# State products and scores of a state attention with an MoE-style layer, moved from 128x32 to 64x32 array tiles

## The chip, the cores and the metric

The kernel runs on one core of a Trainium2 chip. The metric is device time in microseconds (us) of one execution; for the kernel before, three runs are at hand. The profile is one execution recorded by the hardware profiler. PE is the matrix engine (matmuls; PEld is its weight loads), DVE the vector engine, ACT the scalar engine, POOL the general engine; SP issues most DMAs.

## What is computed

For each of 8 batches and 8 heads, 512 tokens `x` and 32 state rows `state` (64 values each) read each other by softmax attention; the 544 results per batch, 512 wide over the heads, go through a layer norm and a two-layer network with a residual.

```python
scores = x @ state.T / 8;          a = softmax(scores);   xread = a @ state      # 512 x 32 per head
scores2 = state @ x.T / 8;         a2 = softmax(scores2); sread = a2 @ x         # 32 x 512 per head
x2 = concat([xread, sread])        # heads side by side: (8, 544, 512)
xn = (x2 - mean) / sqrt(var + 1e-6) * g_ln
out = x2 + relu(xn @ w_ch1) @ w_ch2     # w_ch1 512 x 2048, w_ch2 2048 x 512, both float64 in memory
```

## The kernel before

All operands of large products are split into a high and a low float16 part, and a product is the sum of three of the four part products (`TERMS`). The two weight matrices are loaded as 64-bit words and cut to 32 bits on the chip; they are handled in four units `u` of 512 hidden columns. `weights1(u)` loads w1 (`raw`, 2 DMAs of 1 MB), converts it (`words`), multiplies by the gain and subtracts the column mean, finds a scale and splits (`split`) to float16; four DMAs (`w1c<-raw`) then copy the parts to tile `w1c` so that the high half of a head's 64 rows and the low half lie on the 128 partitions one above the other. `weights2(u)` does the same for w2 and needs no copies.

For a token, `xread` is a softmax row times the 32 state rows, so the first layer is taken through the state: `state_products(b)` (L660) multiplies the state (`sT`, weights in the array) by w1 once per batch, `matrix` = state x w1, 256 rows (8 heads x 32) by 512 columns per unit, and the layer's products then use `matrix` with the softmax numerators `ea`. In `state_products` and in `scores` (L400) the array is cut into four tiles of 128 rows and 32 columns, one for each of four heads `j`; the 128 rows hold a head's high and low halves stacked. For one half `g` of the heads, `a` = 0, 1 (state high, state low) times four heads makes 8 matmuls of 512 columns (L665, L403). Each group writes one PSUM bank from a pool of two (`half`); the bank is evicted by one ACT and one DVE instruction into `matrix`.

`read_state` (L475) does `a2 @ x` with 32 matmuls of 64 columns per batch; since the halves of x lie on separate output rows, ACT copies the result to SBUF and four float32 matmuls with a matrix `fold` (L492) add the halves and turn rows and columns.

For batch 0 the first layer (L701) and second layer (L715) are plain; from batch 1 on they are done with a Strassen-like scheme (`strassen_hidden`, L799, and `strassen_products`, L855) that uses 7 instead of 8 products with combinations of w2 (L747, tile `sums`). The last stage takes the 256 rows of `sread` (all batches) through the same layers (`first_of_state`, L808), for which two DMAs per unit (`high<-w1c`) copy w1's high halves to another layout.

Every piece of work is a step of a numbered stream, and the text `PLAN` lists stream:step pairs in the order in which they are issued; each engine executes its own steps in that order, so a step that waits holds up what stands behind it on its engine. Waits on data and on free tiles are put in by the tile framework. `banks` is a pair of PSUM banks with one buffer, used in a batch by the scale search, `scores`, `read_state` and the mix of token reads (L515). `accumulator` has four banks.

## Time and profile before

| what | value |
|---|---|
| runs | 666.45, 667.62, 667.91 us (median 667.62) |
| profiled execution, span | 665.9 us (the page gives no other time for it) |
| busy: PE, DVE, ACT, POOL | 626.3, 498.0, 388.2, 216.7 us |
| PE busy in 0 to 80 us, in 150 to 620 us | 48.1 of 80, 468.1 of 470 us |
| HBM read and written | 28.05 and 9.44 MB |

The page gives busy times by engine, busy tenths in 40 slices of the span, the chain of work that ended last, groups of like instructions with mean duration and the idle time before them, and DMA issues. The rows on which the argument stands are shown with the prediction. In rows of a group, the two shapes behind a name are the output and the input; for PE, `128*32` is rows times columns of the array that the instruction uses.

### The profile page before, as it was taken

To read this page: it belongs to the slowest core of one execution; us is meant where nothing else is said; L and a number is where in the kernel's file an instruction comes from. 1 tells how busy PE (TensorE), PEld (TensorE's weight loads), DVE (VectorE), ACT (ScalarE), POOL (GpSimd) and SP (SyncE) were. 2 spreads that over 40 slices of the span, in tenths; PEclk is the share of its full clock that TensorE was granted. 3 is DMA by queue.
4 is the path that set the end of the run, shared out by engine and by line. 5 is a ranking of instruction groups with operands and counts; after the bars stand their busy time and mean duration, and the time that the engine had idled before them with its cause. 6 is when DMAs were issued, how large, how long until landed. Compare 5 with 4: busy or idle time off the path is not lost.

```text
span 665.9 us, 14680 instructions
## 1 busy us (share of the span) xinstructions
PE 626.3 (94%) x5948; PEld 493.1 (74%) x5948; DVE 498.0 (75%) x1002; ACT 388.2 (58%) x699; POOL 216.7 (33%) x189
## 2 busy tenths in 40 slices
PE   0676999999999999999999999999999999999996
...
PEclk9977999999999999999999999999999999999998
...
DMA packets 98563, 69.63 MB, mean 105 GB/s; under 512 B 72704, under 2 KB 90624, under 8 KB 98048
## 3 DMA queue, kind: packets, MB, share of 16 engines
...
q10 hardware_dynamic: 1248, 0.79, 0.4%
...
HBM read 28.05 MB, written 9.44 MB: 56 GB/s over the span
## 4 chain that ended last, share of the span: by engine, by line
PE 90%; DVE 5%; DMA 2%; ACT 1%; issue 1%; DVEq 0%; SPq 0%
PE acc L855 41%; PE half L799 22%; PE acc L715 6%; PE half L665 5%; PE acc L701 3%; PE half L808 3%; PE acc L747 2%; PE acc L599 2%; PE banks L403 1%; DVE w_t L186 1%; PE banks L479 1%; PE banks L515 1%; PE banks L492 1%; DMA x_f<-in_x_dram 1%; PE acc L608 1%; DMA w1c<-raw 1%
## 5 line engine op out<-in xcount | busy, mean ns | idle before, releaser
L855 PEld LDWEIGHTS <-xs 128*128 128x128 f16 x2520 | 242.4, 98 | 43.6 <-issue 15.3
L186 POOL TENSOR_TENSOR xs<-rs,xs 128x512 f16<-128x512 f32 x120 | 142.4, 1199 | 272.7 <-ACT xs L186 207.1
L855 PE MATMUL acc<-w2h,xs 128*128 128x256 f16 x1440 | 183.0, 273 | 0.0
L799 PE MATMUL half<-ea,matrix 128*128 128x256 f16 x1344 | 159.4, 273 | 0.0
L799 PEld LDWEIGHTS <-matrix 128*128 128x128 f16 x1344 | 130.7, 98 | 16.6 <-issue 0.8
L855 PE MATMUL acc<-sums,xs 128*128 128x256 f16 x1080 | 141.9, 273 | 0.0
L186 DVE SCALAR_TENSOR_TENSOR rs<-half,rs 128x256 f32<-128x256 f32 x224 | 89.4, 419 | 27.6 <-ACT rs L186 13.3
L186 ACT ACTIVATE xs<-rs 128x512 f16<-128x512 f32 x128 | 77.1, 618 | 40.5 <-DVE rs L186 33.8
L186 ACT ACTIVATE xs<-half 128x256 f16<-128x256 f32 (+1 forms) x112 | 53.6, 487 | 72.5 <-PE half L799 50.5
L186 DVE SCALAR_TENSOR_TENSOR xs<-half,xs 128x256 f16<-128x256 f32 (+1 forms) x112 | 61.2, 550 | 28.1 <-ACT xs L186 24.5
L186 ACT ACTIVATE matrix<-half,hs 128x512 f16<-128x512 f32 x56 | 38.0, 687 | 35.2 <-PE half L665 34.9
L186 DVE SCALAR_TENSOR_TENSOR matrix<-half,hs,matrix 128x512 f16<-128x512 f32 x56 | 41.2, 742 | 16.0 <-ACT matrix L186 15.3
L186 ACT ACTIVATE rs<-half 128x256 f32<-128x256 f32 x56 | 21.3, 381 | 42.5 <-PE half L799 40.1
L715 PE MATMUL acc<-w2h,hid 128*128 128x512 f16 x192 | 43.1, 379 | 0.0
L186 DVE TENSOR_TENSOR strip<-acc,strip 128x256 f32<-128x256 f32 (+1 forms) x60 | 33.2, 554 | 10.5 <-PE acc L855 7.5
L665 PE MATMUL half<-w1c,sT 128*32 128x512 f16 x448 | 33.5, 384 | 1.9 <-DVE rs L186 1.0
L186 POOL TENSOR_TENSOR ts<-ts,mA 128x1024 f32<-128x1024 f32 (+1 forms) x8 | 14.4, 1804 | 60.9 <-DVE mA L186 54.5
L715 PEld LDWEIGHTS <-hid 128*128 128x128 f16 x192 | 18.5, 98 | 20.9 <-issue 0.4
L186 DVE SCALAR_TENSOR_TENSOR x<-x_f,x_s,x 128x512 f16<-128x512 f32 x32 | 24.8, 798 | 5.3 <-ACT x L186 5.3
L186 DVE BATCH_NORM_STATS2 s<-xr 128x6 f32<-128x512 f32 x32 | 21.6, 684 | 8.7 <-ACT xr L186 8.6
L186 ACT ACTIVATE x<-x_f,x_s 128x512 f16<-128x512 f32 x32 | 21.7, 713 | 9.8 <-DVE x_s L186 9.8
L186 POOL TENSOR_TENSOR hid<-strip,hid 128x512 f16<-128x512 f32 x16 | 18.5, 1170 | 26.6 <-ACT hid L186 26.5
(152 smaller groups left out, 770.1 us busy)
## 6 DMA issues: line engine op xcount, KB each, us to landing
raw<-in_moe_w_ch_dram SPq DMA_DIRECT2D x9, 1024.0 KB, 7.3
out_dram<-xr SPq DMA_DIRECT2D x16, 512.0 KB, 3.0
x_f<-in_x_dram SPq DMA_DIRECT2D x15, 512.0 KB, 5.6
sums<-in_moe_w_ch_dram SPq DMA_DIRECT2D x7, 1024.0 KB, 8.2
...
ek<-ek SPq DMA_DIRECT2D x7, 512.0 KB, 4.3
xr<-part POOLq DMA_DIRECT2D x6, 512.0 KB, 5.0
w1c<-raw SPq DMA_DIRECT2D x8, 256.0 KB, 5.1
```

The lines of the kernel that those rows point to most:

```text
L186: return lambda: f(*map(now, args), **{k: now(v) for k, v in kw.items()})
L403: nc.tensor.matmul(o[32 * j:32 * j + 32], lhsT=sT[:, g, a, 32 * j:32 * j + 32], rhs=xT[:, s, 4 * g + j].rearrange("p c t -> p (c t)"), sta ...
L479: nc.tensor.matmul(ps_z[:, h // 4, :, h % 4], lhsT=xv[:, c // hc, h, c % hc], rhs=ebT[:, :, h // 4, c, 32 * (h % 4):32 * (h % 4) + 32], st ...
L492: nc.tensor.matmul(pr[:, g], lhsT=z4[:, g, i], rhs=fold, start=i == 0, stop=i == 1, skip_group_check=True)
L599: nc.tensor.matmul(ps, lhsT=gm[:, k:k + 1].broadcast_to([P, P]), rhs=t4[:, k], start=k == 0, stop=k == 3)
L665: nc.tensor.matmul(ps[32 * j:32 * j + 32], lhsT=sT[:, g, a, 32 * j:32 * j + 32], rhs=w[:, 2 * g + j // 2, j % 2], start=a == 0, stop=a == ...
L701: nc.tensor.matmul(o[:, 256 * f:256 * f + 256], lhsT=m[:, g, i, P * (q + f):P * (q + f) + P], rhs=ea[:, s, k, g], start=f == 0 and g == 0 ...
L715: nc.tensor.matmul(po, lhsT=hid[:, i, q, c * P:(c + 1) * P], rhs=w[:, j, q], start=first and q == 0 and n == 0, stop=last and q == 3 and n ...
L747: nc.tensor.matmul(o, lhsT=signs[:, k // 2], rhs=v[k], start=start and k == 0, stop=k == 3, skip_group_check=True)
L799: nc.tensor.matmul(ps[:, 256 * q:256 * q + 256], lhsT=m[:, h, i, P * (2 * k + q):P * (2 * k + q) + P], rhs=ea[:, 0, j, h, 256 * g:256 * g ...
L808: nc.tensor.matmul(ps[:, 256 * q:256 * q + 256].rearrange("p (t n) -> p t n", t=2), lhsT=w[:, k // 2, k % 2, fs] if k < H else wn[:, k - H ...
L855: nc.tensor.matmul(po[o], lhsT=y[:, n, i, o] if o < 2 else x[:, o - 2, n, i], rhs=v[j], start=u == 0 and n == 0 and k == 0 and o in (2, 1, ...
```

## The change

Row halves. w1's rows now come in by head half: partitions 0 to 63 hold heads 0 to 3, partitions 64 to 127 heads 4 to 7. Each raw load becomes two DMAs of 64 partitions (8 more DMAs in all), the gain is loaded in two pieces, and `split` writes `w1c` directly: the 16 copies `w1c<-raw` and `w1c<-sums` and the 8 copies `high<-w1c` are gone. `x16` and `xT` take the same layout; the state's `sT` is built with one ACT and one DVE instruction in place of one and two.

Tiles. `scores` and `state_products` use tiles of 64 rows and 32 columns: 8 tiles (two row halves `g`, four columns `j`), three sets of part products, 24 matmuls of 512 columns for what took 16 in four sets. The two halves `g` write different PSUM banks. From batch 1 on the products of a unit are taken into the pair `banks` instead of two tiles of `half`, and are evicted by one ACT and one DVE instruction of 1024 columns.

State reads. `read_state` uses 48 matmuls (three part products summed in PSUM), then ACT and DVE copy 64 partitions each to SBUF, and one float32 transpose on PE takes the place of the four float32 products.

Order. `PLAN` is a new table throughout. Three places follow.

On DVE in the start-up, the rows up to the first units of `matrix` of batch 0 (`ts`, `dA`, `ef` and `ea` belong to the softmax, `raw`, `sums` and `w1c` with `w1_t` are the low parts of w1's units, `w1_t` with `gx` the gain and mean). Before:

```order
L186 SCALAR_TENSOR_TENSOR raw_147<-w1_t_155,of_weights_216,raw_147 128x2048
L186 SCALAR_TENSOR_TENSOR raw_247<-w1_t_183,of_weights_216,raw_247 128x2048
L186 SCALAR_TENSOR_TENSOR w1_t_351<-w1_t_351,gx_77,acc_424 128x512 x4
L186 TENSOR_REDUCE dA_241<-ts_205 128x16
L186 TENSOR_SCALAR dA_241<-dA_241 128x16
L186 SCALAR_TENSOR_TENSOR sums_70<-w1_t_139,of_weights_216,sums_70 128x2048
L186 RECIPROCAL dA_241<-dA_241 128x16
L186 SCALAR_TENSOR_TENSOR matrix_470<-acc_440,matrix_470 128x512
```

Now:

```order
L192 SCALAR_TENSOR_TENSOR w1c_294<-w1_t_160,of_weights_247,w1c_294 128x2048
L192 TENSOR_TENSOR ts_251<-ts_251,dA_308 128x512
L192 STREAM_TRANSPOSE ef_342<-ts_251 128x512
L192 SCALAR_TENSOR_TENSOR w1_t_314<-w1_t_314,gx_77,acc_319 128x512
L192 TENSOR_REDUCE dA_308<-ts_251 128x16
L192 TENSOR_SCALAR dA_308<-dA_308 128x16
L192 RECIPROCAL dA_308<-dA_308 128x16
L192 SCALAR_TENSOR_TENSOR ea_381<-ef_342,ea_381 128x512
L192 SCALAR_TENSOR_TENSOR matrix_385<-acc_346,matrix_385 128x512
L192 SCALAR_TENSOR_TENSOR matrix_385<-acc_347,matrix_385 128x512
```

Before, three units of w1 are split ahead of the first `matrix`; now one is, and the other two stand some ten rows behind it.

On SP's queue in the start-up, the w1 loads up to the first transposes. Before:

```order
L186 DMA s_j_75<-in_state_dram 128x2x64
L585 DMA sums_70<-in_moe_w_ch1_dram 128x2x1024 x2
L585 DMA raw_147<-in_moe_w_ch1_dram 128x2x1024
L585 DMA raw_157<-in_moe_w_ch1_dram 128x2x1024
L585 DMA raw_173<-in_moe_w_ch1_dram 128x2x1024
L186 DMA_TRANSPOSE xT_178<-x16_108 128x16x128
```

Now:

```order
L192 DMA s_j_75<-in_state_dram 128x2x64
L584 DMA sums_70<-in_moe_w_ch1_dram 64x2x1024 x4
L584 DMA raw_137<-in_moe_w_ch1_dram 64x2x1024 x2
L584 DMA raw_152<-in_moe_w_ch1_dram 64x2x1024 x2
L584 DMA raw_164<-in_moe_w_ch1_dram 64x2x1024 x2
L584 DMA raw_180<-in_moe_w_ch1_dram 64x2x1024 x2
L192 DMA_TRANSPOSE sT_0_198<-sh_96 128x2x128
```

Six megabytes in twelve DMAs, before five in five, go out ahead of the first transpose.

On DVE in a later batch, around evictions of `matrix` (`rs` and `xs` are the Strassen combinations). Before:

```order
L186 SCALAR_TENSOR_TENSOR eb<-eB,eb 128x1024
L186 SCALAR_TENSOR_TENSOR matrix<-half,hs,matrix 128x512
L186 SCALAR_TENSOR_TENSOR xs<-half,xs 128x2x256
L186 TENSOR_REDUCE dA<-ts 128x32
L186 TENSOR_SCALAR dA<-dA 128x32
L186 RECIPROCAL dA<-dA 128x32
L186 SCALAR_TENSOR_TENSOR matrix<-half,hs,matrix 128x512 x2
```

Now, at a place where two units follow each other closely:

```order
L192 SCALAR_TENSOR_TENSOR matrix<-banks,hs,matrix 128x2x512
L192 TENSOR_SCALAR ux<-x_i 128x1
L192 SCALAR_TENSOR_TENSOR rs<-half,rs 128x256 x2
L192 SCALAR_TENSOR_TENSOR xr<-strip,of_second,xr 128x512
L192 SCALAR_TENSOR_TENSOR matrix<-banks,hs,matrix 128x2x512
```

One instruction of 1024 columns from `banks` stands for two of 512 from `half`, and the next unit's products wait for it, since the pair has one buffer.

The diff (of the table two rows are shown; where `...` stands, lines that follow from these are left out):

```diff
--- before.py
+++ after.py
-    "1:0 1:3-4 1:1-2 1:5-12 4:1 1:19 1:72 0:0 4:6 1:20 1:24-25 4:5 4:7 4:0 4:3 1:17-18 4:2 4:4 3:1 3:6 1:22-23 "
+    "0:0 1:4 1:3 1:2 1:1 1:0 1:5-11 4:0-1 1:13 1:12 1:18 1:71 2:0 1:14 1:23 1:21 4:2-3 1:19 1:24 1:22 4:6 4:4-5 2:1 "
...
-            yield do(engines[hh].dma_start, out=xf[:, hs], in_=src[:, hs])
+            o, i = (xf[:, hh], src[:, :, 2 * hh:2 * hh + 2]) if b == 0 else (xf[:, 0, hs], src[:, hs])
+            yield do(engines[hh].dma_start, out=o, in_=i)
...
-        sT = fixed([P, G, 2, P], F16, f"sT_{b % 2}")
-        yield do(nc.scalar.activation, sh[:, :, 0], sj.unsqueeze(2).broadcast_to([P, G, 2, D]), AF.Copy, scale=sst)
-        for i in range(2):
-            yield do(nc.vector.scalar_tensor_tensor, sh[:, :, 1, i], sj, sst, sh[:, :, 0, i], ALU.mult, ALU.subtract)
-        yield do(nc.sync.dma_start_transpose, out=sT.rearrange("p g a n -> p (g a) n"),
-                 in_=sh.rearrange("p g a i d -> p (g a i d)"))
-
-        xT = (rows("xT") if b > 0 else unit(3, "xT")).bitcast(F16).rearrange("p (s h c t) -> p s h c t", s=parts, h=H, c=hc)
-        xTa = xT.rearrange("p s h c t -> p (s h c) t")
+        sT = fixed([P, 2, P], F16, f"sT_{b % 2}")
+        yield do(nc.scalar.activation, sh[:, 0], sj, AF.Copy, scale=sst)
+        yield do(nc.vector.scalar_tensor_tensor, sh[:, 1], sj, sst, sh[:, 0], ALU.mult, ALU.subtract)
+        yield do(nc.sync.dma_start_transpose, out=sT, in_=sh.rearrange("p i g d -> p (i g d)"))
...
-        def scores(s, g, o, sT, xT):
-            for a in range(2):
+        def scores(s, ps, sT, xT):
+            for n, (a, i) in enumerate(TERMS):
                 for j in range(4):
-                    nc.tensor.matmul(o[32 * j:32 * j + 32], lhsT=sT[:, g, a, 32 * j:32 * j + 32],
-                                     rhs=xT[:, s, 4 * g + j].rearrange("p c t -> p (c t)"),
-                                     start=a == 0, stop=a == 1, skip_group_check=True)
-
-        psv = ps if parts == 1 else ps.rearrange("p s (g t) -> p g s t", g=G)
-        eB = quad("eB").rearrange("p (g s t) -> p g s t", g=G, s=parts)
+                    for g in range(G):
+                        k = hc * (4 * s + j)
+                        nc.tensor.matmul(ps[32 * j:32 * j + 32, g, w * s:w * s + w],
+                                         lhsT=sT[D * g:D * g + D, a, 32 * j:32 * j + 32],
+                                         rhs=xT[D * g:D * g + D, k:k + hc, i], start=n == 0, stop=n == 2,
+                                         skip_group_check=True)
...
         def read_state(ps_z, x16, ebT):
-            xv = x16.rearrange("p (s h c) i d -> p s h c (i d)", s=parts, c=hc)
-            for h in range(H):
+            for j in range(4):
                 for c in range(C):
-                    nc.tensor.matmul(ps_z[:, h // 4, :, h % 4], lhsT=xv[:, c // hc, h, c % hc],
-                                     rhs=ebT[:, :, h // 4, c, 32 * (h % 4):32 * (h % 4) + 32],
-                                     start=c == 0, stop=c == C - 1, skip_group_check=True)
+                    a = hc * (4 * (c // hc) + j) + c % hc
+                    for n, (i, k) in enumerate(TERMS):
+                        nc.tensor.matmul(ps_z[:, j], lhsT=x16[:, a, i], rhs=ebT[:, k, :, c, 32 * j:32 * j + 32],
+                                         start=c == 0 and n == 0, stop=c == C - 1 and n == 2, skip_group_check=True)
         yield do(read_state, ps_z, x16, ebT)
-        z = halves("z").bitcast(F32)[:, 0:512]
-        z4 = z.rearrange("p (g i n) -> p g i n", g=G, i=2)
-        pr = pz[:, 1, 0:G * D].rearrange("p (g d) -> p g d", g=G)
+        z = halves("z").bitcast(F32)[:, 0:P]
+        pr = pz[:, 1, 0:G * D]
         sread = fixed([P, G, D], F32, "sread")
-        yield do(nc.scalar.activation, z, pz[:, 0], AF.Copy)
-
-        def fold_halves(pr, z4):
-            for g in range(G):
-                for i in range(2):
-                    nc.tensor.matmul(pr[:, g], lhsT=z4[:, g, i], rhs=fold, start=i == 0, stop=i == 1,
-                                     skip_group_check=True)
-        yield do(fold_halves, pr, z4)
-        yield do(nc.vector.tensor_tensor, sread, pr, rB.unsqueeze(2).broadcast_to([P, G, D]), ALU.mult)
+        for g, copy in enumerate((partial(nc.scalar.activation, func=AF.Copy), nc.vector.tensor_copy)):
+            r = slice(D * g, D * g + D)
+            yield do(copy, z[r].rearrange("p (j n) -> p j n", j=4), ps_z[r, :, g])
+        yield do(nc.tensor.transpose, pr, z, idf)
+        yield do(nc.vector.tensor_tensor, sread, pr.rearrange("p (g d) -> p g d", g=G),
+                 rB.unsqueeze(2).broadcast_to([P, G, D]), ALU.mult)
...
-            nc.sync.dma_start(out=raw.rearrange("p (k f) -> p k f", k=2),
-                              in_=w1[256 * fh:256 * fh + 256, 1024 * u:1024 * u + 1024].rearrange("(k p) f -> p k f",
-                                                                                                  p=P))
+            rows_of = w1[:, 1024 * u:1024 * u + 1024].rearrange("(g j d) f -> g d j f", g=G, j=4)
+            for g in range(G):
+                nc.sync.dma_start(out=raw[D * g:D * g + D].rearrange("p (k f) -> p k f", k=2),
+                                  in_=rows_of[g, :, 2 * fh:2 * fh + 2])
...
-        hl = raws[1].bitcast(F16).rearrange("p (i e) -> p i e", i=2)
-        yield from split(hl[:, 0], hl[:, 1], t, scale)
-        hl = hl.rearrange("p i (k f) -> p i k f", k=4)
-        w = narrow(u, "w1c").bitcast(F16).rearrange("p (k s f) -> p k s f", k=4, s=2)
-        w1c[u] = w
-        for i in range(2):
-            for s in range(2):
-                to = 64 * (i ^ s)
-                yield do(nc.sync.dma_start, out=w[to:to + 64, :, s], in_=hl[64 * s:64 * s + 64, i])
+        w = narrow(u, "w1c").bitcast(F16).rearrange("p (i e) -> p i e", i=2)
+        yield from split(w[:, 0], w[:, 1], t, scale)
+        w1c[u] = w.rearrange("p i (j f) -> p i j f", j=4)
...
-        def multiply(ps, g, sT, w):
-            for a in range(2):
+        def multiply(ps0, ps1, sT, w):
+            for n, (a, i) in enumerate(TERMS):
                 for j in range(4):
-                    nc.tensor.matmul(ps[32 * j:32 * j + 32], lhsT=sT[:, g, a, 32 * j:32 * j + 32],
-                                     rhs=w[:, 2 * g + j // 2, j % 2], start=a == 0, stop=a == 1, skip_group_check=True)
+                    for g in range(G):
+                        nc.tensor.matmul((ps0, ps1)[g][32 * j:32 * j + 32],
+                                         lhsT=sT[D * g:D * g + D, a, 32 * j:32 * j + 32],
+                                         rhs=w[D * g:D * g + D, i, j], start=n == 0, stop=n == 2, skip_group_check=True)
         sT = results[b][1]
         for u in range(U):
             m = matrix[b][u] = block(4, f"matrix_{u}", 1, "matrix").bitcast(F16).rearrange("p (g i f) -> p g i f", g=G, i=2)
-            for g in range(G):
-                ps = accumulator() if b == 0 else half()
-                scale = CM if b == 0 else hs[:, u:u + 1]
-                yield do(multiply, ps, g, sT, w1c[u])
-                yield do(nc.scalar.activation, m[:, g, 0], ps, AF.Copy, scale=scale)
-                yield do(nc.vector.scalar_tensor_tensor, m[:, g, 1], ps, scale, m[:, g, 0], ALU.mult, ALU.subtract)
+            scale = CM if b == 0 else hs[:, u:u + 1]
+            if b == 0:
+                ps = [accumulator() for _ in range(G)]
+                todo = [(ps[g], m[:, g, 0], m[:, g, 1]) for g in range(G)]
+            else:
+                two = banks()
+                ps = [two[:, g] for g in range(G)]
+                todo = [(two, m[:, :, 0], m[:, :, 1])]
+            yield do(multiply, *ps, sT, w1c[u])
+            for v, hi, lo in todo:
+                yield do(nc.scalar.activation, hi, v, AF.Copy, scale=scale)
+                yield do(nc.vector.scalar_tensor_tensor, lo, v, scale, hi, ALU.mult, ALU.subtract)
...
-                def first_of_state(ps, j, w, wn, xsT):
+                def first_of_state(ps, k, w, xsT):
                     for q in range(2):
-                        fs = slice(P * (2 * j + q), P * (2 * j + q) + P)
-                        for k in range(12):
-                            nc.tensor.matmul(ps[:, 256 * q:256 * q + 256].rearrange("p (t n) -> p t n", t=2),
-                                             lhsT=w[:, k // 2, k % 2, fs] if k < H else wn[:, k - H, fs], rhs=xsT[:, :, k],
-                                             start=q == 0 and k == 0, stop=k == 11, skip_group_check=True)
+                        fs = slice(P * (2 * k + q), P * (2 * k + q) + P)
+                        for n, (i, a) in enumerate(TERMS):
+                            for j in range(4):
+                                nc.tensor.matmul(ps[:, 256 * q:256 * q + 256].rearrange("p (t n) -> p t n", t=2),
+                                                 lhsT=w[:, i, j, fs], rhs=xsT[:, :, 4 * a + j],
+                                                 start=q == 0 and n == 0 and j == 0, stop=n == 2 and j == 3,
+                                                 skip_group_check=True)
...
-    def high_halves(u):
-
-        high[u] = quad("high").bitcast(F16).rearrange("p (k f) -> p k f", k=4)
-        for s in range(2):
-            half = slice(64 * s, 64 * s + 64)
-            yield do(nc.sync.dma_start, out=high[u][half], in_=w1c[u][half, :, s])
+    state_rows_T = [None]
...
```

81 lines of the change are left out of this document (41 added, 40 removed), and 243 rows, old and new, of the table PLAN.

## Prediction, written before the changed kernel was run

> **What bounds the kernel now.** I read the page's busy times and slices first, then the stretches, then single rows on PE.
>
> ```profile
> PE 626.3 (94%) x5948; PEld 493.1 (74%) x5948; DVE 498.0 (75%) x1002; ACT 388.2 (58%) x699; POOL 216.7 (33%) x189
> PE   0676999999999999999999999999999999999996
> PEclk9977999999999999999999999999999999999998
> 0.00:20.00 20.00, 4.58 (x8) 2.16 (x9) 12.66 (x30) 10.21 (x16) 0.70 (x6) 1.00 0.92 325
> 20.00:40.00 20.00, 14.35 (x61) 5.91 (x59) 18.40 (x32) 11.72 (x13) 0.00 (x0) 0.83 1.00 321
> 40.00:60.00 20.00, 12.02 (x118) 6.80 (x118) 18.92 (x27) 17.26 (x22) 1.05 (x1) 0.79 0.89 199
> 60.00:80.00 20.00, 17.18 (x173) 11.86 (x172) 17.44 (x38) 17.34 (x29) 5.59 (x5) 0.87 0.89 248
> 150.00:620.00 470.00, 468.12 (x4753) 391.91 (x4746) 354.51 (x737) 261.13 (x507) 172.55 (x144) 1.00 0.32 78
> ```
>
> In a stretch's row, busy time stands in the order PE, PEld, DVE, ACT, POOL, then granted clock, DMA share and GB/s. From 80 us on PE is the bound: 468.1 of 470 us in the long stretch, at clock 1.00, with DVE at 75% and ACT at 56% there. Before 80 us PE lies idle 31.9 us (80 less 48.1), while DVE is busy 67.4 of 80. So two currencies count: PE time taken out of the steady part, at face value as long as the other engines follow; and in the start-up the time at which DVE has prepared enough for PE.
>
> **Tiled products.** This piece of PE's timeline shows what a tiled step costs.
>
> ```profile
> 214.15 0.62 PE L665 MATMUL half<-w1c,sT 128*32 128x512 f16 x8
> 214.70 1.48 PE L855 MATMUL acc<-w2h,xs 128*128 128x256 f16 x12
> 216.02 0.82 PE L855 MATMUL acc<-sums,xs 128*128 128x256 f16 x6
> 216.77 0.62 PE L665 MATMUL half<-w1c,sT 128*32 128x512 f16 x8
> 217.32 1.11 PE L479 MATMUL banks<-ebT,x 128*128 128x64 f16 x32
> 218.35 0.61 PE L665 MATMUL half<-w1c,sT 128*32 128x512 f16 x8
> ...
> 86.50 1.05 PE L665 MATMUL half<-w1c,sT 128*32 128x512 f16 x16
> 87.48 1.49 PE L701 MATMUL acc<-ea,matrix 128*128 128x256 f16 x12
> ```
>
> Eight tiled matmuls, two sets of four side by side, hold PE for 0.55 us (214.15 to 214.70). Sixteen without a break hold it 0.98 us (86.50 to 87.48), so a further set costs (0.98-0.55)/2 = 0.215 us. An ordinary matmul takes 1.32/12 = 0.11 us; after the six at 216.02 the next should start at 216.68 and starts at 216.77, so entering costs 0.09. A run of s sets costs 0.64+0.215(s-2).
>
> From batch 1 on there are 56 steps of state products and 14 of scores, 70 of two sets; by the order of issue they stand in 47 runs of one step, 10 of two and 1 of three: 47x0.64 + 10x1.07 + 1.50 = 42.3 us. The change has 28 and 7 steps of three sets; 34 stand alone and one follows a step of batch 0: 34x0.855 + 0.65 = 29.7 us, if eight tiles run side by side. Term: -12.6 us. If the two row halves take turns, a step has six sets: 34x1.50 + 1.29 = 52.3 us, +10.0.
>
> Which of the two? The trace has no 64-row tiles, but it has 32-row ones, in batch 0's mix:
>
> ```profile
> 43.52 0.96 PE L530 MATMUL acc<-sh,ea 32*128 32x64 f16 x34 [1.01 <-DVE ea L186]
> 48.24 0.52 PE L530 MATMUL acc<-sh,ea 32*128 32x64 f16 x12
> ```
>
> A step is 12 matmuls on one row group, and the next step takes the next group. One record lasts 0.19, so twelve on one group start every (0.52-0.19)/11 = 0.030 us, while 34 over three groups start every (0.96-0.19)/33 = 0.023. At a change of group they do overlap, each group into a bank of its own, as the change has it too. I take eight tiles side by side. 24 starts in 3x0.215 us need one each 0.027, a little under the single group's 0.030, so some 0.1 us a step (3.5 us in all) may be lost; I take none, and keep it in the range.
>
> [...]
>
> **State reads.** Rows for the products with `fold`, and for the nearest float32 transpose:
>
> ```profile
> 225.46 1.00 PE L492 MATMUL banks<-fold,z 128*128 128x64 f32 x8
> 226.30 2.78 PE L799 MATMUL half<-ea,matrix 128*128 128x256 f16 x24
> ...
> 241.64 0.27 PE L186 MATMUL banks<-idf,x_am 128*2 128x128 f32 x1
> 241.75 0.82 PE L855 MATMUL acc<-sums,xs 128*128 128x256 f16 x6
> ```
>
> 32 matmuls at 217.32 take 1.03 us with the entry, so (1.03-0.09)/32 = 0.029 each, and 16 more cost 0.47 per batch: +3.3 us over seven. The `fold` products hold PE 0.84 us. A transpose of 2 columns holds it 0.11; one of 128 columns is no cheaper and, with a weight load in the open, no dearer than two to three `fold` passes (0.105 each): 0.11 to 0.30, I take 0.20, as its moving side equals the row's and only the load is longer. 7x(0.20-0.84) = -4.5 us (-5.1 to -3.8). ACT and DVE now copy 64 partitions side by side where ACT copied 512 columns; PE has other products between, so nothing on the path; uncovered, about what the old copy cost, so nothing either.
>
> **Evictions and the pair `banks`.** The state products move from two single banks to the one pair.
>
> ```profile
> 613.18 1.10 ACT L186 ACTIVATE xr<-banks,ux 128x1024 f32<-128x1024 f32 x1
> 37.05 1.22 DVE L186 SCALAR_TENSOR_TENSOR eb<-eB,eb 128x1024 f16<-128x1024 f32 x1 [0.44 <-ACT eb L186]
> 274.72 0.61 PE L665 MATMUL half<-w1c,sT 128*32 128x512 f16 x8 [0.96 <-DVE rs L186]
> ```
>
> A pair is free again after 1.10 on ACT and 1.22 on DVE, 2.3 us plus what stands ahead in their queues. By the order of issue the least PE work between a state product and the next user of the pair is 24 matmuls, 2.6 us, at two places, and 3.3 or more elsewhere; before the mix (1.10 to free) it is 2.0. That covers it narrowly. PE waits in order, so what queues behind such a step is all Strassen work, and ACT and DVE then wait for that. On the other side the first layer no longer shares `half` with state products, which cost 0.96 us once at 274.72. Together 0 to +8 us; I take +1.
>
> **Start-up.** The copies go, and DVE's order changes.
>
> ```profile
> 57.85 1.90 PE L665 MATMUL acc<-w1c,sT 128*32 128x512 f16 x16 [3.68 <-DMA w1c<-raw]
> 65.36 2.74 PE L701 MATMUL acc<-ea,matrix 128*128 128x256 f16 x12
> 83.82 2.75 PE L715 MATMUL acc<-w2h,hid 128*128 128x512 f16 x12
> ...
> 49.53 4.61 DVE L186 SCALAR_TENSOR_TENSOR raw<-w_t,of_weights,raw 128x2048 f16<-128x2048 f32 x2
> 54.06 2.72 DVE L186 SCALAR_TENSOR_TENSOR w_t<-w_t,gx,acc 128x512 f32<-128x512 f32 x4
> 59.92 0.63 DVE L186 SCALAR_TENSOR_TENSOR matrix<-acc,matrix 128x512 f16<-128x512 f32 x1
> 80.62 1.27 DVE L186 SCALAR_TENSOR_TENSOR w2h<-w_t,of_weights,w2h 128x1024 f16<-128x1024 f32 x1
> ...
> L186 DVE BATCH_NORM_STATS2 s<-xr 128x6 f32<-128x512 f32 x32 | 21.6, 684 | 8.7 <-ACT xr L186 8.6
> ```
>
> PE's first state product waited 3.68 us for a copy. In the new order only one split of 2.3 us and one of the four rows with `gx` stand ahead of the first `matrix`, where three splits and four rows stood: 59.92 less 4.6 less 2.0 gives 53 us, and the first layer (L701) can start near 55 instead of 65. But the other two splits then come before the next units, so PE waits again. What lets PE run without a break is the first half of w2 (`w2h`, done at 81.9): ahead of its last row the new order has one split less (-2.3), one fewer DVE row for `sh`, and about three BATCH_NORM rows more (0.68 each, +2.0). So L715 moves by 0 to -3 us, and PE enters its full stretch about 2 us earlier. Term: -2. If the 10 us at the first layer carry through it is -8.
>
> The price against it lies in the loads, which come in pieces of 64 partitions.
>
> ```profile
> raw<-in_moe_w_ch_dram SPq DMA_DIRECT2D x9, 1024.0 KB, 7.3
> out_dram<-xr SPq DMA_DIRECT2D x16, 512.0 KB, 3.0
> ek<-ek SPq DMA_DIRECT2D x7, 512.0 KB, 4.3
> w1c<-raw SPq DMA_DIRECT2D x8, 256.0 KB, 5.1
> ```
>
> 512 KB to 64 partitions (`ek`) took 4.3 us, 512 KB from 128 partitions 3.0; 1.3 us for each of 16 loads is at most 21 us of queue time. Against it, 16 copies of 256 KB (4 MB, 13 us at 320 GB/s) leave the same queue, and DVE, not a load, sets the pace. So I take no loss; the outer bound is +8 after the copies' gain. Transposes from a smaller `sh`, the gain in two pieces and the `high` copies near the end lie beside PE's work and cost nothing; uncovered, a small DMA is 2 to 3 us once.
>
> [...]
>
> **The sum.** Made against the profiled execution's span: 665.9 - 12.6 + 3.3 - 4.5 + 1 - 2 = 651.1 us. The median of the runs lies 1.7 above that span, so 652.8, say 653.
>
> **Rivals.** (a) The row halves take turns on PE. The term -12.6 becomes +10.0, so 653+22.6 = 676, slower. For it: no 64-row tile in the trace; against it: the overlap at L530. It decides from five sets a step: 34x(0.64+0.215x3)+1.07 = 44.8 us is 2.5 more than before, which eats the 1.2 of the reads and most of the start-up. (b) The order at the pair `banks` makes PE wait: 28 state products and 21 other users, 0.2 us each is +9, so 661. For it: 2.6 us of cover against 2.3; against it: only a few places are that tight. (c) The halves of w1 land late, +8 instead of -2: 663. For it: the 4.3 against 3.0; against it: the copies' 4 MB. (d) The early first layer carries through: 647. For it: PE idles 31.9 us in the start-up; against it: DVE has nearly as much to do before `w2h`.
>
> **How the numbers follow.** Forecast 0.60, (a) 0.07, (b) 0.12, (c) 0.08, (d) 0.13. About 0.2% (1.3 us) is what a measurement tells from no change. All but (a) are faster; some of (b) and (c) can add up to no change or to a loss: faster 0.89, same 0.03, slower 0.08. The forecast's own range is 648 to 658 (reads, entry and pair at their bounds); with (b), (c), (d) and some of each, 644 to 664.
>
> **What would show it.** A state product of 24 matmuls that holds PE 0.77 us (start to the next start) shows side by side; 1.4 shows turns. PE's idle time from 80 us to the end should stay under 3 us; waits of PE on `banks` above that show (b). The first L701 near 55 us and L715 near 82 show the start-up; ACT's waits for `raw` DMAs above 5 us in sum show (c). PE's busy time in all should fall to about 613 us. The forecast is wrong if tiled rows fall by less than 8 us, or if DVE's order leaves PE idle again between 80 and 150 us, where its work now comes earlier.

## The result, and the profile after

The changed kernel took 708.53 us (median of 4 runs, 708.02 to 709.76) against 667.52 us for the kernel before in the same sitting (666.45 to 667.91): a ratio of 1.0617 with a 95% interval of 1.0601 to 1.0632, slower by 6%. The prediction was 653 us, faster by 2%: the time moved the other way, and 708.5 us lies outside even its widest range (644 to 664). The profiled execution has a span of 706.2 us, 40.3 more than before.

The page of the kernel after, its busy times and slices:

```profile
PE 626.5 (89%) x6348; PEld 494.0 (70%) x6348; DVE 501.7 (71%) x974; ACT 372.9 (53%) x671; POOL 223.1 (32%) x189
PE   0546989989999999999889998999899999999995
```

PE's busy time is what it was, but its slices are no longer a row of nines, and the nines set in later. Two views say how much of this is start-up and how much a leaking steady part. The stretches 5 to 45 us and 180 to 640 us, before:

```profile
5.00:45.00 40.00, 20.30 (x104) 9.22 (x105) 35.27 (x64) 24.68 (x29) 0.00 (x0) 0.91 1.01 334
180.00:640.00 460.00, 458.12 (x4613) 383.13 (x4612) 344.44 (x701) 247.99 (x471) 171.34 (x143) 1.00 0.32 78
```

The same stretches after:

```profile
5.00:45.00 40.00, 16.71 (x58) 6.68 (x59) 24.93 (x41) 15.07 (x18) 0.00 (x0) 0.99 1.05 219
180.00:640.00 460.00, 435.38 (x4736) 363.59 (x4735) 338.18 (x674) 233.43 (x446) 164.33 (x137) 0.99 0.30 69
```

In the long stretch PE lay idle for 1.9 us before and lies idle for 24.6 after. In the first stretch the DMA engines are as full as before (share 1.05) but move 219 GB/s instead of 334. And PE's timeline, of the kernel after:

```profile
70.22 0.58 PE L701 MATMUL acc<-ea,matrix 128*128 128x256 f16 x2
97.39 0.38 PE L715 MATMUL acc<-w2h,hid 128*128 128x512 f16 x1
...
184.79 0.82 PE L857 MATMUL acc<-w2h,xs 128*128 128x256 f16 x6
185.54 0.84 PE L658 MATMUL banks<-w1c,sT 64*32 64x512 f16 x24
186.31 0.39 PE L747 MATMUL acc<-w2h,signs 128*128 128x256 f16 x2
```

The first layer starts at 70.2 us (before 65.4), the second at 97.4 (before 83.8). A state product of 24 tiled matmuls holds PE 0.77 us (185.54 to 186.31). Entering it costs 0.09 us more: the six matmuls at 184.79 take 0.66 us (0.11 each), and the product starts at 185.54 and not at 185.45.

From the starts of PE's matmuls I made an account that is used for all runs below. From the first L715 on, a matmul's distance to the next start is work up to what its kind takes back to back, and a wait beyond that (excesses under 0.03 us are not counted).

| kernel | first L715 | work after it | waits after it | last start on PE |
|---|---|---|---|---|
| before | 83.8 | 573.1 | 2.9 | 659.8 |
| after | 97.4 | 559.1 | 42.3 | 699.5 |
| difference | +13.6 | -14.0 | +39.4 | +39.7 |

(Small excesses make up the other 0.7 us of the last column; the tail behind PE's last matmul is 0.6 us longer.) The work fell as predicted. The loss has two parts: a start-up of +13.6 us, and waits of +39.4 us, of which 15.1 stand at `half<-ea,matrix` (L799), 15.7 at the users of the pair `banks` (L481 5.0, L658 4.6, L407 3.1, L512 3.0) and the rest at many small places.

What ended PE's waits is in the profile. Four rows of PE's waits from 97.39 us on, of the kernel after (total us, times, longest):

```profile
PE half L799 <- DVE xs L192: 7.8, 8, 2.8
PE banks L481 <- DVE matrix L192: 3.5, 2, 2.1
PE banks L407 <- DMA xT<-x: 2.8, 3, 1.9
PE banks L658 <- DVE matrix L192: 2.8, 2, 2.2
```

These rows count idle time alone, so they are smaller than the account. At the users of the pair, a step that emptied the pair ended 7.7 us of idle time (`matrix` 6.3, `sread` 0.7, `eB` 0.7), and a transfer ended 5.7 (`xT` 2.8, `ek` 1.9, `ebT` 1.0). So not all of the 15.7 us is the pair's.

A part of what the account calls waits is a lower clock. In this stretch, just behind PE's wait that ends at 439.39 us, the granted clock is 0.50:

```profile
439.80:443.20 3.40, 3.40 (x18) 2.39 (x17) 1.92 (x4) 1.38 (x2) 1.55 (x1) 0.50 0.30 57
```

Two more such stretches of 3.4 us begin at 153.1 and 535.4 us, each behind a wait of 1.6 to 2.1 us. In the one at 439.80 PE started 18 products, one per 0.19 us instead of 0.11. At half the speed the three cost at most 5.1 us, an estimate (half of three times 3.4). The kernel before has clock 1.00 from 70 to 660 us. That the waits bring the lower clock about was not tested by itself, and waits of 1.9 and 2.2 us that end at 495.1 and 512.5 us are not followed by one; but the reordered kernel of part 4, with few waits, has 1.00 from 70 to 670 us.

### The profile page after: what moved, and what is told of

It is laid out like the page before. It is cut to its first block, busy times and chain, and to the rows that moved or that the text cites. A ratio compares the mean times of both kernels' runs of the same rounds, so it can differ in the third digit from the quotient of the medians.

```text
span 706.2 us, 15380 instructions
## 1 busy us (share of the span) xinstructions
PE 626.5 (89%) x6348; PEld 494.0 (70%) x6348; DVE 501.7 (71%) x974; ACT 372.9 (53%) x671; POOL 223.1 (32%) x189
## 5 line engine op out<-in xcount | busy, mean ns | idle before, releaser
L799 PE MATMUL half<-ea,matrix 128*128 128x256 f16 x1344 | 162.9, 274 | 11.0 <-DVE xs L192 7.8
L799 PEld LDWEIGHTS <-matrix 128*128 128x128 f16 x1344 | 129.8, 98 | 32.9 <-DVE xs L192 7.3
L192 ACT ACTIVATE xs<-rs 128x512 f16<-128x512 f32 (+1 forms) x128 | 76.9, 620 | 70.9 <-DVE rs L192 66.0
L192 ACT ACTIVATE xs<-half 128x256 f16<-128x256 f32 (+1 forms) x112 | 53.3, 487 | 67.8 <-DVE rs L192 33.4
L192 DVE SCALAR_TENSOR_TENSOR xs<-half,xs 128x256 f16<-128x256 f32 (+1 forms) x112 | 60.6, 548 | 32.4 <-ACT xs L192 29.3
L715 PE MATMUL acc<-w2h,hid 128*128 128x512 f16 x192 | 43.3, 379 | 0.1
L192 DVE SCALAR_TENSOR_TENSOR matrix<-banks,hs,matrix 128x1024 f16<-128x1024 f32 x28 | 35.5, 1269 | 8.1 <-ACT matrix L192 8.0
L192 ACT ACTIVATE matrix<-banks,hs 128x1024 f16<-128x1024 f32 x28 | 31.1, 1112 | 8.8 <-PE banks L658 8.3
L192 POOL TENSOR_TENSOR hid<-strip,hid 128x512 f16<-128x512 f32 x16 | 24.2, 1547 | 31.2 <-ACT hid L192 31.2
L715 PEld LDWEIGHTS <-hid 128*128 128x128 f16 x192 | 18.5, 98 | 21.4 <-issue 1.1
L597 PE MATMUL acc<-w_t,gm 128*128 128x512 f32 x32 | 19.0, 742 | 15.5 <-DVE w_t L192 15.5
L701 PE MATMUL acc<-ea,matrix 128*128 128x256 f16 x192 | 27.2, 299 | 4.1 <-DVE of_weights L192 2.0
L192 DVE SCALAR_TENSOR_TENSOR x<-x_f,x_s,x 128x512 f16<-128x512 f32 x32 | 26.9, 863 | 1.4 <-ACT x L192 1.4
L658 PE MATMUL banks<-w1c,sT 64*32 64x512 f16 x672 | 23.7, 379 | 4.1 <-DVE matrix L192 2.8
```

Of the source, the lines that this page charges most:

```text
L192: return lambda: f(*map(now, args), **{k: now(v) for k, v in kw.items()})
L597: nc.tensor.matmul(ps, lhsT=gm[:, k:k + 1].broadcast_to([P, P]), rhs=t4[:, k], start=k == 0, stop=k == 3)
L658: nc.tensor.matmul((ps0, ps1)[g][32 * j:32 * j + 32], lhsT=sT[D * g:D * g + D, a, 32 * j:32 * j + 32], rhs=w[D * g:D * g + D, i, j], start ...
L701: nc.tensor.matmul(o[:, 256 * f:256 * f + 256], lhsT=m[:, g, i, P * (q + f):P * (q + f) + P], rhs=ea[:, s, k, g], start=f == 0 and g == 0 ...
L715: nc.tensor.matmul(po, lhsT=hid[:, i, q, c * P:(c + 1) * P], rhs=w[:, j, q], start=first and q == 0 and n == 0, stop=last and q == 3 and n ...
L799: nc.tensor.matmul(ps[:, 256 * q:256 * q + 256], lhsT=m[:, h, i, P * (2 * k + q):P * (2 * k + q) + P], rhs=ea[:, 0, j, h, 256 * g:256 * g ...
```

## Experiments

All were timed beside the kernel before on the same chip (its medians there 667.6 to 668.4 us); the ratios are to that.

**1. Is it the pair, or the order?** The theory from the two traces was that the new order leaks and the pair as such costs little; the rival, that the pair makes PE wait in any order. The first run keeps the changed code and takes before's order, step for step, as far as the steps have a counterpart (only `PLAN` differs, from its first row):

```diff
-    "0:0 1:4 1:3 1:2 1:1 1:0 1:5-11 4:0-1 1:13 1:12 1:18 1:71 2:0 1:14 1:23 1:21 4:2-3 1:19 1:24 1:22 4:6 4:4-5 2:1 "
+    "1:0 1:3-4 1:1-2 1:5-12 4:1 1:18 1:71 0:0 4:6 1:19 1:23-24 4:5 4:7 4:0 4:3 1:16-17 4:2 4:4 3:1 3:6 1:21-22 "
```

> All new code, but the table of the order is that of the kernel before, step for step (where one new step stands for two, at the later of the two; 29 steps moved by up to 37 places so that the one pair of banks is never asked for twice). First theory: the new order makes ACT, DVE and PE wait for one another, and so PE lost 39 us in waits after the start-up. Then these waits fall from 42.3 us to under 8, and the time to 708.5 - 36 = about 672, and some 5 us less if the start-up gets better too, since here the gain's step comes after the x reductions (667). Rival: the one pair of banks, which state products now need, makes the waits; it is still there, so PE still loses 30 us or more and the time stays above 695.

It took 758.06 us, 1.1353 (1.1333 to 1.1373), with 82.6 us of waits, 61.8 of them at the users of `banks`. From its waits, PE's own on `banks` (total us, times, longest):

```profile
PE banks L651 <- DVE matrix L185: 14.9, 8, 2.6
PE banks L474 <- DVE matrix L185: 12.7, 5, 2.6
PE banks L505 <- DVE matrix L185: 8.7, 4, 2.6
```

PE stands at the pair until DVE, the second of its two evictors, has let go. The evictors come at once here: from a state product's first matmul to the end of DVE's eviction it is 3.3 us in the median of 28 products and 5.2 at most. The next user of the pair stands closer than that. In an order made for two single banks the pair is the dearest thing in the kernel. The next run gives the state products of the later batches two single banks of `half` again, in that same order, each unit's product placed where both are free:

```diff
-            if b == 0:
-                ps = [accumulator() for _ in range(G)]
-                todo = [(ps[g], m[:, g, 0], m[:, g, 1]) for g in range(G)]
-            else:
-                two = banks()
-                ps = [two[:, g] for g in range(G)]
-                todo = [(two, m[:, :, 0], m[:, :, 1])]
+            ps = [accumulator() if b == 0 else half() for _ in range(G)]
+            todo = [(ps[g], m[:, g, 0], m[:, g, 1]) for g in range(G)]
```

> As the first run (order of the kernel before, new code, w1 loaded by head half), but the state products of batches 1 to 7 write two single banks of the pool half, where the kernel before had them, and not the pair of banks; ACT and DVE evict 512 columns at a time. In the first run PE lost 82.6 us in waits after L715 began, 61.8 of them on users of the pair. If the one pair is what makes PE wait, the waits fall to 3 to 15 us and the time from 758 to 672 to 688 (the late start-up, L715 at 101, is still in it). Rival: the old order does not suit the new code whatever the bank: the waits stay over 40 us and the time above 710.

701.32 us, 1.0509 (1.0476 to 1.0542); waits 31.9 us, 50.7 less, but not the 3 to 15 that were expected. So with before's order the rival of the first run held: the pair, with its users where they stand there, cost some 50 us. But the changed kernel has another order, with only 15.7 us at the pair, and what the pair costs at best was still open.

**2. The start-up: the loads.** Three edits try to give w1 back the rate it had before (334 GB/s in 5 to 45 us), one moves a small load. The first kept the heads where the change puts them and loaded two heads at a time to all 128 partitions, the source with an outermost dimension of 2:

```diff
-            rows_of = w1[:, 1024 * u:1024 * u + 1024].rearrange("(g j d) f -> g d j f", g=G, j=4)
-            for g in range(G):
-                nc.sync.dma_start(out=raw[D * g:D * g + D].rearrange("p (k f) -> p k f", k=2),
-                                  in_=rows_of[g, :, 2 * fh:2 * fh + 2])
+            rows_of = w1[:, 1024 * u:1024 * u + 1024].rearrange("(g j d) f -> j g d f", g=G, j=4)
+            for k in range(2):
+                nc.sync.dma_start(out=raw[:, 1024 * k:1024 * k + 1024],
+                                  in_=rows_of[2 * fh + k])
```

> The changed kernel with the two loads of each half of a unit of w1 cut by another line: each brings one of the two row blocks to all 128 partitions (4 KB each) instead of both to 64 partitions (8 KB each). Same data, same bytes, same number of transfers, same order. Theory: a transfer to 64 partitions moves at most at half the rate, so the rate from 5 to 45 us rises from 218 GB/s to 330 or more, the last raw lands some 10 us earlier, L715 starts at 88 to 92 and the time is 699 to 704. Rival: the head of DVE's order or the order itself sets the start-up: the rate rises but the time stays at 706 to 709. Second rival: the number of transfers sets the rate, and it stays near 218.

It failed as a mend: 832.62 us, 1.2462 (1.2442 to 1.2481). Its stretch from 5 to 45 us:

```profile
5.00:45.00 40.00, 0.92 (x3) 0.57 (x3) 5.67 (x16) 4.74 (x9) 0.00 (x0) 1.00 0.17 59
```

The engines were nearly idle (share 0.17) and moved 59 GB/s. In 8 to 28 us, where little else is under way, the share is 0.13. What holds these loads back, no run shows. The run is of use all the same: the second layer started at 224.1 us and the waits after it were 39.0 us, little less than the 42.3 of the change. So a late start only shifts the rest; the waits are not its consequence. The same loads with before's order gave 881.72 us, 1.32 (1.3181 to 1.322), and told nothing more:

> The order of the kernel before with the new code (as the first run) and w1 loaded by row blocks to 128 partitions (as the third). If order and loads are both at fault and nothing else, the sum of the prediction is left: about 651 to 656 us, faster than both kernels. If the pair of banks is at fault: above 685.

The second edit leaves the head halves and gives them a queue each:

```diff
-                nc.sync.dma_start(out=raw[D * g:D * g + D].rearrange("p (k f) -> p k f", k=2),
+                (nc.sync, nc.scalar)[g].dma_start(out=raw[D * g:D * g + D].rearrange("p (k f) -> p k f", k=2),
```

> The changed kernel with each pair of loads of w1's halves on two queues, SP's for partitions 0 to 63 and ACT's for 64 to 127, so that transfers to both halves can be on their way at once. If a transfer to 64 partitions is bounded by what one half of the partitions can take in, the rate from 5 to 45 us rises from 219 GB/s to above 300, and the time falls by 4 to 9 us to 699 to 704. If it is bounded by the descriptors of such a load, the rate stays within 10% of 219 and the time within 2 us of 708.

711.23 us, 1.0654 (1.0598 to 1.0709), from only two runs, 708.29 and 714.16. Its stretch from 5 to 45 us:

```profile
5.00:45.00 40.00, 13.89 (x23) 5.28 (x23) 17.10 (x30) 10.37 (x15) 0.00 (x0) 0.96 1.06 198
```

198 GB/s with all engines full: no gain from a second queue, and the second layer starts at 106.3 us. By the words of the expectation that speaks for the descriptors as the bound; of the cause no run shows more than the packets, below. The third puts other heads on the halves. With even heads on partitions 0 to 63 and odd ones on 64 to 127, heads 2k and 2k+1 are 128 consecutive rows of w1, and one DMA of 128 partitions brings 1 MB:

```diff
-            for g in range(G):
-                nc.sync.dma_start(out=raw[D * g:D * g + D].rearrange("p (k f) -> p k f", k=2),
-                                  in_=rows_of[g, :, 2 * fh:2 * fh + 2])
+            nc.sync.dma_start(out=raw.rearrange("p (k f) -> p k f", k=2),
+                              in_=w1[256 * fh:256 * fh + 256, 1024 * u:1024 * u + 1024].rearrange("(k p) f -> p k f", p=P))
...
-            v = xf[:, k, 4 * g:4 * g + 4] if parts == 2 else xf[:, 0, 4 * g + 2 * k:4 * g + 2 * k + 2]
+            v = xf[:, k, g:g + 7:2] if parts == 2 else xf[:, 0, 4 * k + g:4 * k + g + 3:2]
...
-                                         lhsT=ek[:, h // 4, h % 4, (2 * t + c) * P:(2 * t + c + 1) * P],
+                                         lhsT=ek[:, h % 2, h // 2, (2 * t + c) * P:(2 * t + c + 1) * P],
```

(The state's rows and the columns of the state reads are taken in the same arrangement, and the gain comes in one load.) The order of the changed kernel is kept:

> The changed kernel (its own order, its pair of banks) with only the even and odd heads in w1's row halves, so that each load goes to 128 partitions. The raw of w1 lands in 7 to 10 us instead of 15.2, the rate from 5 to 45 us is above 300 GB/s. Loads at fault for the start-up: L715 at 86 to 91 instead of 97.4, waits after it unchanged at 38 to 43 us, time 698 to 703. Rival, the wait for the gain and the order at fault: L715 within 2 us of 97.4, time 706 to 709.

692.22 us, 1.0375 (1.0351 to 1.0399), 16 us better than the change and better than the 698 to 703 expected. Its stretch from 5 to 45 us, and then its PE:

```profile
5.00:45.00 40.00, 19.05 (x86) 7.51 (x87) 32.52 (x60) 22.34 (x25) 0.00 (x0) 0.98 0.93 319
```

```profile
83.73 0.59 PE L716 MATMUL acc<-w2h,hid 128*128 128x512 f16 x2 [0.21 <-ACT strip L194]
```

319 GB/s, and the second layer starts at 83.7 us, 13.7 earlier than in the change and level with before. From the DMA issues, first of the changed kernel, then of this one (KB each, median us from issue to landing):

```profile
raw<-in_moe_w_ch_dram SPq DMA_DIRECT2D x10, 512.0 KB, 15.2
```

```profile
raw<-in_moe_w_ch_dram SPq DMA_DIRECT2D x9, 1024.0 KB, 7.5
```

Half the bytes took twice as long, the time behind other loads in the queue included. The packets in the traces show it without the queue: these loads are moved in packets of 4096 bytes in all four kernels, and between 8 and 28 us one takes 312 ns (median) in the change, 291 with two queues, 164 in this run and 159 in the kernel before. So the halves are not slow because their packets are smaller; each packet moves at about half the rate, while the engines count as busy (share 1.05 in the change, 1.06 with two queues). Over 5 to 45 us the halves gave 219 and 198 GB/s and the full width 319 to 334, so in the stretch the halves' rate was about two thirds and not the half that the first edit's theory set. Why a packet to 64 partitions takes about twice as long, no run shows. Waits after the second layer's start are 40.3 us, near the 42.3 without the edit: the two parts of the loss are separate. The edit also brings the gain in one load, and DVE's wait for it falls from 12.1 to 5.7 us; what each of the two is worth alone, no run shows.

The small load: the gain in two pieces stands at the head of DVE's queue. In the changed kernel's timeline:

```profile
13.84 0.17 DVE L192 TENSOR_SCALAR gm<-gx 128x4 f32<-128x4 f32 x1 [12.13 <-DMA gx<-in_moe_g_ln_dram]
```

DVE lies idle for 12.1 of its first 13.8 us. Step `0:0` moved behind the first loads and conversions:

```diff
-    "0:0 1:4 1:3 1:2 1:1 1:0 1:5-11 4:0-1 1:13 1:12 1:18 1:71 2:0 1:14 1:23 1:21 4:2-3 1:19 1:24 1:22 4:6 4:4-5 2:1 "
+    "1:4 1:3 1:2 1:1 1:0 1:5-11 4:0-1 1:13 1:12 1:18 1:71 2:0 1:14 1:23 1:21 0:0 4:2-3 1:19 1:24 1:22 4:6 4:4-5 "
```

> The changed kernel with one step of the order moved: the product of the gain (which waits for the load of gx until 13.8 us) comes behind the x reductions and the scale steps instead of ahead of them. Theory: the wait at the head of DVE's order is 6 us of the 13.6 us by which the start-up got later; the second layer (L715) starts at 91 instead of 97, the time is 702 to 704. Rival: the loads of w1 set the pace anyway, so DVE waits for them instead: L715 within 1.5 us of 97.4 and the time 707 to 709.

705.56 us, 1.0559 (1.0533 to 1.0585): 3 us better than the change (0.8 at the second layer's start, 2.6 in the waits behind it), between the two expectations. DVE waits elsewhere instead: in its first 60 us 8.1 us for `raw`, where it waited 2.7 in the change, and 6.3 for `s_j`, where it did not wait. So the slow loads take most of the 12.1 us back.

**3. Both pieces in the old order.** Even and odd heads together with the two banks of `half`:

> As the run with the two single banks, and w1's row halves hold the even and the odd heads instead of heads 0 to 3 and 4 to 7: then a unit's rows lie in the order of the input, and one load brings them to 128 partitions, as in the kernel before, with no copies either. If the loads to 64 partitions are what makes the start-up late, the first state product comes at 55 to 60 instead of 70, L715 at 80 to 86 instead of 101, and the time is 652 to 668: as fast as the kernel before or faster. Rival: the start-up is late because of the order of DVE and ACT: L715 stays after 95 and the time is within 5 us of the run with the two single banks.

689.14 us, 1.0322 (1.0294 to 1.035); second layer at 86.0, waits 30.3. The start-up is mended, and the steady part still leaks 30 us, so the time is 21 us above the expected range. Neither bank layout was rid of it under an order made for another kernel.

**4. The order alone.** What do PE's waits in the changed kernel look like? One place in the steady part, rows of ACT, DVE and PE from the timeline of the kernel after (start, us, engine, instruction; in brackets the idle time before it and what ended it):

```profile
430.71 0.78 ACT L192 ACTIVATE eB<-banks,mB,es 128x512 f32<-128x512 f32 x1 [3.65 <-DVE ts L192]
431.49 0.77 ACT L192 ACTIVATE eB<-banks,mB,es 128x512 f32<-128x512 f32 x1
432.37 1.06 ACT L192 ACTIVATE eb<-eB 128x1024 f16<-128x1024 f32 x1
432.39 0.84 PE L658 MATMUL banks<-w1c,sT 64*32 64x512 f16 x24
433.34 0.37 ACT L192 ACTIVATE rs<-half 128x256 f32<-128x256 f32 x1
...
434.08 2.66 DVE L192 SCALAR_TENSOR_TENSOR eb<-eB,eb 128x1024 f16<-128x1024 f32 x1
436.66 1.33 DVE L192 SCALAR_TENSOR_TENSOR rs<-half,rs 128x256 f32<-128x256 f32 x3
438.02 0.60 ACT L192 ACTIVATE xs<-half 128x512 f16<-128x512 f32 x1 [4.04 <-DVE rs L192]
438.65 0.69 DVE L192 SCALAR_TENSOR_TENSOR xs<-half,xs 128x512 f16<-128x512 f32 x1 [0.66 <-ACT xs L192]
439.39 1.95 PE L799 MATMUL half<-ea,matrix 128*128 128x256 f16 x10 [2.78 <-DVE xs L192]
439.55 1.11 ACT L192 ACTIVATE matrix<-banks,hs 128x1024 f16<-128x1024 f32 x1
444.77 1.24 DVE L192 SCALAR_TENSOR_TENSOR matrix<-banks,hs,matrix 128x1024 f16<-128x1024 f32 x1
```

The next batch's softmax (`eB`, `eb`) stands in ACT's and DVE's order ahead of the evictions of `half`. ACT waits 3.65 us for DVE's `ts`, then does `eB` and `eb` before it comes to `half`. DVE does `eb` for 2.66 us before the next `rs` out of `half`, ACT waits 4.04 us for that `rs`, and PE waits 2.78 us for a bank. The state product of 432.39 shares this fate: ACT evicts it at 439.55, DVE at 444.77, and the pair is free at 446.01, 13.6 us after the product's start. In the stretch from 180 to 640 us DVE is busy 74% of the time and ACT 51%; there is time enough, but the wrong step comes first. The theory was that an order made for this kernel, with the changed code as it is, removes most of the waits; the order was chosen with durations measured in the traces. The first attempt (`PLAN` from about 97 us on):

> The changed kernel word for word, except for the order of its steps from the second layer of batch 0 on (about 97 us): there the steps of PE, ACT, DVE and POOL were put in another order, chosen with the durations that the changed kernel's own trace shows, so that a step stands where what it reads is ready and a state product where the pair of banks is free. The code, the loads, the pair of banks and the start-up stay. Theory: the changed kernel's order is what makes PE wait, and the pair alone does not force it: PE's waits after L715 fall from 42.3 to 5 to 15 us, L715 stays at 97 to 98, the time falls to 669 to 682. Rival: with one pair for 28 state products and 38 other users no order avoids the waits: they stay above 25 us and the time above 690.

698.63 us, 1.0459 (1.0436 to 1.0481), waits 31.7: a miss, on the rival's side of both bounds. PE's groups show where it leaked (busy, mean ns, idle before and what ended it):

```profile
L411 PE MATMUL banks<-xT,sT 64*32 64x512 f16 (+1 forms) x216 | 7.3, 356 | 10.4 <-DMA sT<-sh 5.8 <-DMA xT<-x 3.0 <-DVE ts L196 1.6
```

The scores wait 10.4 us, 8.8 of them for the transposing transfers `xT` and `sT`; in the changed kernel they wait 3.1, 2.8 of them for `xT`. (The mix waits 6.2 us more, for `s_r` and `ek`.) What such a transfer does to SP, on SP's timeline of a sister run (this new order with even and odd heads, below):

```profile
255.84 5.72 SPq L196 DMA_TRANSPOSE xT<-x  x2
261.61 1.25 SPq L196 DMA_TRANSPOSE sT<-sh  x1
```

Two `xT` held SP for 5.72 us, `sT` for 1.25, and in the changed kernel a plain transfer holds it for 0.38 to 0.61 in the median of its kind (1.9 at most); what stood behind the two `xT` in SP's order was issued later (`sT` at 261.61). The first new order had left this out. That sister run, and the two banks of `half` with a new order of their own, also taken without SP's time:

> As the run before, with w1's row halves holding even and odd heads, so that its loads go to 128 partitions (the start-up of that run: L715 at 83.7). Both causes are then taken away: 83.7 + 559.5 us of PE's work + 5 to 15 of waits + 6.5 behind PE's end = 655 to 665 us: faster than the kernel before, and about what was predicted. If a cause is still missing: above 672.

> As the run before, but the state products of batches 1 to 7 in two banks of the pool half, with an order chosen for that. PE's work is 3 us more (562.5). If the pair is the scarcer place, waits fall to 1 to 10 us and the time is 656 to 664; if half, which the first layer needs all the time, is the scarcer one, waits stay above 20 us and the time above 675.

682.71 us, 1.0213 (1.0187 to 1.0239), waits 32.4; and 700.86 us, 1.0475 (1.0435 to 1.0516), waits 40.6, worse than with the old order. Then the same with SP's time counted. The changed kernel, nothing altered but `PLAN`; the steps from the first difference on, ranges written out:

```diff
-    14:3 5:20 17:34 13:4 11:1 6:15 41:2 17:25 14:2 11:6 14:4 11:4 18:3 11:5 10:9 10:10
+    1:67 17:25 5:20 14:3 7:46 11:1 17:34 11:4 13:4 7:39 14:4 14:2 6:15 10:9 13:5 14:6
```

> The changed kernel word for word, again with another order of its steps from about 97 us on, like e9. What e9's trace showed is taken in: a transposing transfer holds SP's queue for 1.2 to 3.6 us (so the next transfer is late) and lands 3 us after that, so the casts and transposes of x stand earlier and in a row ahead of the scores. Theory (the order makes PE wait, not the pair): PE's waits after L715 fall from 42.3 (e9: 31.7) to 5 to 12 us, the time to 670 to 677. Rival (the pair forces them): they stay above 25 us, the time above 690.

674.02 us, 1.0097 (1.0072 to 1.0122), as the theory expected: 34.5 us less than the change, by order alone. Waits 9.6 us. (This order differs from the first new one at many places, so what SP's time alone is worth is not shown.) Its long stretch:

```profile
180.00:640.00 460.00, 457.82 (x5000) 390.41 (x4998) 346.41 (x698) 242.51 (x459) 178.37 (x145) 1.00 0.30 72
```

PE idles 2.2 us of 460 where it idled 24.6. The same place of the program, where a softmax and the evictions of `half` meet, in its timeline:

```profile
404.25 0.78 ACT L197 ACTIVATE eB<-banks,mB,es 128x512 f32<-128x512 f32 x1 [2.72 <-DVE mB L197]
405.02 0.59 ACT L197 ACTIVATE xs<-half 128x512 f16<-128x512 f32 x1
406.01 0.39 ACT L197 ACTIVATE xs<-half 128x256 f16<-128x256 f32 x1 [0.41 <-PE half L804]
406.30 0.38 ACT L197 ACTIVATE rs<-half 128x256 f32<-128x256 f32 x1
406.56 0.78 ACT L197 ACTIVATE eB<-banks,mB,es 128x512 f32<-128x512 f32 x1
407.87 0.84 PE L663 MATMUL banks<-w1c,sT 64*32 64x512 f16 x24
408.65 2.97 PE L804 MATMUL half<-ea,matrix 128*128 128x256 f16 x24
```

ACT still waits 2.72 us in front of `eB`, but three evictions stand between the two `eB`, and PE goes on without a gap: the state product of 407.87 holds it to 408.64, and the next products start at 408.65. The groups of PE's products into the pair and into `half`, changed kernel first, then this one:

```profile
L799 PE MATMUL half<-ea,matrix 128*128 128x256 f16 x1344 | 162.9, 274 | 11.0 <-DVE xs L192 7.8 <-ACT xs L192 1.8 <-DVE rs L192 1.2
L658 PE MATMUL banks<-w1c,sT 64*32 64x512 f16 x672 | 23.7, 379 | 4.1 <-DVE matrix L192 2.8 <-DVE sread L192 0.7 <-ACT eB L192 0.7
```

```profile
L804 PE MATMUL half<-ea,matrix 128*128 128x256 f16 x1344 | 160.8, 273 | 0.9 <-DVE matrix L197 0.5 <-DVE xs L197 0.3
L663 PE MATMUL banks<-w1c,sT 64*32 64x512 f16 x672 | 23.6, 379 | 1.2 <-ACT eB L197 1.2
```

The state products, which by the account waited 31.9 us for the pair in the first run, wait 1.2 here. Yet the pair is not held for less time: from a state product's first matmul to the end of DVE's eviction it is 4.9 us in the median of 28 here (11.5 at most) and 4.9 in the changed kernel (14.1 at most). The pair does not force the waits; the order decides where its next user stands. The same treatment for the two banks of `half` (with even and odd heads) tells which bank layout is better once each has an order of its own:

> As e13, with the state products of batches 1 to 7 in two banks of half and an order chosen for that, with each where both are free. PE's work is 562.5 us, L715 at 86. If two free banks at the right moment are all a tiled state product needs, whichever pool they come from, waits fall from 30.3 (e6) to 1 to 8 us: 655 to 663. Rival: half is needed by the first layer so often that waits stay above 20: above 674.

671.91 us, 1.0054 (1.0036 to 1.0073), second layer at 85.9 and waits 16.8, of which 9.4 at `half<-ea,matrix`. Between the two expectations. The next run, with the pair, is 9.6 us faster; 3.6 of them lie in the start-up, which here has the order of the kernel before, and the rest mostly in the waits (16.8 against 11.2). So with these orders the pair is the better place for the state products; with one search for each layout that is a sign and no proof.

**5. Both parts mended.** The changed kernel with even and odd heads and an order of its own, SP's time counted:

> As e12, with w1's row halves holding even and odd heads (loads to 128 partitions, L715 at 83 to 84). Theory: order and loads are all that went wrong, so the prediction's sum is left: 83.7 + 559.5 + 5 to 10 + 6.5 = 655 to 660 us, faster than the kernel before by 1.2% or more. If something else is missing from the account: above 668.

662.28 us, 0.9919 (0.9896 to 0.9942): 0.8% faster than the kernel before. Second layer at 82.3, waits 11.2, of which 9.4 lie between 83 and 150 us; that is 2.3 us above what was expected. A third order with that stretch in view:

> As e13, with the order from about 80 us on chosen once more, now with the durations of e13's own trace. 9.4 of the 11.2 us that PE waits in e13 lie between 83 and 150 us, where the last weights are made ready beside batch 0 and batch 1. If these waits too are the order's, they fall to 2 to 6 us and the time from 662.3 to 655 to 659, at the prediction's 653 but for 2 to 6 us. If they are set by the loads and splits of w2, the time stays within 2 us of 662.

660.49 us, 0.989 (0.9871 to 0.991), 1.1% faster than before and the best version found; the expectation was missed by 1.5 us. At 1.8 us below the run before it, it is inside the 2 us that the rival gave (loads and splits of w2 set these waits), so the rival is not ruled out. From its page, the busy times:

```profile
PE 611.5 (93%) x6346; PEld 488.9 (74%) x6348; DVE 503.3 (76%) x974; ACT 374.3 (57%) x671; POOL 234.4 (36%) x189
```

Second layer at 83.6, work 558.6, waits 10.3 us, about half of them before 150 us, where it was 9.4: the order took some of these waits away, and others came behind 150 us.

## Why the prediction was wrong, step by step

**Tiled products, state reads, transpose: right.** Predicted together -13.8 us (-12.6, +3.3, -4.5), measured -14.0 in PE's work after the first L715. The single terms hold as well. A state product holds PE the 0.77 us that "What would show it" named for eight tiles side by side, so rival (a) is out; with 0.09 for the entry it is 0.86 us, where the sum had 0.855. The products of the state reads hold PE 1.40 us per batch where they held it 0.93, +3.3 us in seven batches. The transpose holds it 0.11 us where the `fold` products held it 0.84, -5.1 in seven, the lower end of the range given. PE's busy time was to fall to about 613 us: it did so (611.5) only once the waits were gone, because a record of PE lasts longer than the distance to the next start (0.27 us against 0.11 for a product of 256 columns), so that busy time takes in short waits. From the first L715 on it is 571.9 us in the changed kernel, for 559.1 of work, and 561.8 for 558.6 in the last run.

**Start-up: wrong, and the mechanism of rival (c).** The term was -2 us with an outer bound of +8; it is +13.6. The step that failed is "DVE, not a load, sets the pace". I had the row that spoke against it (`ek`, 512 KB to 64 partitions, 4.3 us against 3.0), priced it as 1.3 us a load, and set the copies' 4 MB against it. What this left out is the rate: w1 came at 219 GB/s with the engines full, against 334 before (a packet of 4096 bytes took 312 ns against 159), and DVE had 24.9 us of work in 5 to 45 us instead of 35.3. The marker for (c), ACT's waits for `raw` above 5 us, is in the trace of after, from its waits in the first 100 us:

```profile
ACT raw L192 <- DMA raw<-in_moe_w_ch_dram: 10.0, 3, 3.6
```

With full-width loads the second layer starts at 83.7 us, so my -2 did not come even then; with the new orders it starts at 82.3 and 83.6, a gain of 1.5 and 0.2. The first layer, expected near 55 us and at 70.2 in the change, starts at 57.7 with them, and at 57.5 in the last run. That brought nothing at L715, as the argument against rival (d) had it.

**The pair and the order: wrong by far.** The term was +1 us (0 to +8), rival (b) +9; the waits rose by 39.4. The step that failed is "That covers it narrowly... Together 0 to +8 us; I take +1". It had two faults. First, I compared PE's work between two users of the pair (2.6 us) with the durations of the two evictions (2.3 us), and left "what stands ahead in their queues" without a number. Counted from the product's first matmul, 0.77 and 2.3 us would make 3.1; it was 3.3 us at the least, but 4.9 in the median and 14.1 at most, and 13.6 at the place shown in part 4. (Rival (b) also counted 21 other users of the pair. The code has 35 from batch 1 on, since the scale search takes it once in each batch and the mix twice.) Even so the idle time that the pair made was about what rival (b) gave it, 7.7 us. The larger fault is the second: I looked at the pair alone, though the table was new throughout. That PE time counts "at face value as long as the other engines follow" was a condition, and for it I had no term: 15.1 us of the waits stand at `half`, which I had expected to gain, 5.7 us of idle time at the pair's users were ended by transfers, and up to 5.1 us is the lower clock. That this was the order and not the code, the run with the second new order shows (9.6 us of waits). ACT's waits for DVE's `rs` show it too (33.4 of the 99.4 us after stand in front of an eviction, `xs<-half`, the rest in front of `xs<-rs`). Total us, times, longest, before:

```profile
ACT xs L186 <- DVE rs L186: 48.3, 54, 2.7
```

After:

```profile
ACT xs L192 <- DVE rs L192: 99.4, 68, 4.7
```

In the reordered kernel of part 4 (the second new order):

```profile
ACT xs L197 <- DVE rs L197: 55.1, 56, 2.7
```

The condition I wrote at the end ("if DVE's order leaves PE idle again between 80 and 150 us") named the place too narrowly: only some 5 us of PE's idle time lie there, 24.6 in 180 to 640.

**The sum as a whole.** It was not the size of the change's gain that was misjudged, but the two losses, put at +1 and at nothing: of the 55.5 us between 653 and 708.5, the waits make 38.4 (42.3 less 2.9 and 1), the start-up 15.6 (97.4 less 81.8), and the last 1.5 are excesses too small to be counted, the tail and the distance from span to median. With both mended the kernel takes 660.5, 7.5 above the prediction. By the same account 6.4 of these are waits (10.3 instead of 2.9 and 1), 1.8 the start-up, less 0.7 of work. Whether some order removes those waits, or whether the changed kernel cannot go below them, stays open: the three orders with the pair that count SP's time left 9.6 to 11.2 us, and no run tells the two apart.
